# K and V loads whose 128 reads of 49152 B are each written as two pieces of 24576 B

## The chip, the core and the metric

The kernel runs on one core of a Trainium2 chip. The metric is the device time of one execution in microseconds (us); lower is better. The core has a matrix engine (PE, TensorE), VectorE (DVE), ScalarE (ACT), GpSimd (POOL) and SyncE (SP), each with an instruction stream of its own, and 16 DMA engines that move data between the chip's memory (HBM) and the on-chip memory of 128 partitions (SBUF). SP issues nearly all DMAs of this kernel.

## The reference

Two attention blocks, A and B, do the same thing on inputs of their own, and their outputs are joined along the last axis. Each takes one query token for each of 2 batch entries, and a cache of 8192 keys and values for each of 32 heads of width 192, in bf16.

```python
def _B_ref(x, k_cache, v_cache, wq, wo):
    B, Sq, D = x.shape                 # 2, 1, 640
    H, Dh = 32, 192                    # caches: 2 x 32 x 8192 x 192
    q = (x @ wq).reshape(B, Sq, H, Dh).transpose(0, 2, 1, 3)
    scores = jnp.einsum("bhqd,bhkd->bhqk", q, k_cache) * (Dh ** -0.5)
    p = _softmax(scores, axis=-1)
    o = jnp.einsum("bhqk,bhkd->bhqd", p, v_cache)
    return o.transpose(0, 2, 1, 3).reshape(B, Sq, H * Dh) @ wo
```

(Block A repeats its keys over head groups by a factor of one, so it is the same computation.) Nearly all of the data are the four caches: 4 x 2 x 32 x 8192 x 192 elements of 2 bytes, 805 MB, each read once.

## The kernel before

The work is cut into 64 steps, called pairs here after their two heads: a step takes two neighbouring heads of one batch entry of one block. The keys of two heads are one contiguous stretch of 6 MB (6,291,456 B) in HBM, and so are the values. `kv_src` (L189) views the stretch as 128 rows of 24576 elements (49152 B), one for each partition: partition 0 to 63 hold the first head, 64 to 127 the second, each partition with 128 tokens.

**Buffers.** There are three buffers `ring0` to `ring2` of 128 x 24576 bf16 (L138), 6 MB each. Loads take them in turn: `next_slot` (L196) counts 0, 1, 2, 0, ... The query weights `wq` of both blocks come first, then K and V of each pair in turn (the last two pairs have both K ahead of both V), then the output weights `wo` in pieces.

**Loads.** All these loads are issued by SP, in program order, through `load` and `load_on` (L181 to L187). A load waits until its buffer is free, and SP waits with it, so the loads behind it wait too. A K buffer is free once VectorE has made the fourth product from it (the mark `m, i, 3`), a V buffer once TensorE has run its 64 matmuls (the mark `pv, i`):

```python
            free[s] = [("m", i, 3)] if kind == "k" else [("pv", i)]
```

The consumers wait on the load's semaphore, of which each buffer has one (`rsem`), raised by 16 when a load has landed. The last V load is issued as two column halves of 128 x 12288 elements, so that TensorE can begin on the first half.

**A pair's computation.** The query of the two heads is copied to all partitions by a matmul with a selection matrix (L276) and rounded into `qt` (L282, L283). VectorE multiplies K by it in four quarters (`prod`, L291); TensorE sums 12 slices of each quarter into `scps` with an identity matrix (L296), and VectorE reduces the rest into the scores `sc` (L303). The maximum over the head goes through GpSimd (L312), ScalarE takes the exponentials into `pb` with their sums (L324), and TensorE multiplies them with V in 64 matmuls (L336). The division and the placing of the result (L359 to L379) follow in the next pair. Twelve matmuls on `filler` (L344) do no work that is used; they fill the time in which TensorE waits. The output projection (L394) comes after the last pair.

**Order.** Each engine has a list of operations (`_Stream`) with marks that others wait for, written out in the order of the program; 57 of the 64 pairs run in a loop of 19 turns of three pairs. SP's list is not in a loop.

Of the kernel before, what the change touches and what calls it, by code (L numbers as in the profile page):

```python
# [100 lines left out]
def build_kernel(nc, blocks, out):  # L101
# [15 lines left out]
    DC = D // 128  # L117
    N = Hn * Dh
    RW = T * Dh
    QC = 512  # L120
    NQC = N // QC
    NH2 = D // 2
# [5 lines left out]
    def pair(i):  # L128
        blk, r = divmod(i, B * PB)
        b, ii = divmod(r, PB)  # L130
        return blk, b, ii

    with ExitStack() as es:
# [3 lines left out]

        ring = [sb(f"ring{i}", [128, RW], BF16) for i in range(3)]  # L138
        prod = [sb(f"prod{i}", [128, TQ * Dh], BF16) for i in range(2)]
# [28 lines left out]
        reg = {}  # L168
        S_sp = _Stream("sp", sem("s_sp"), reg)
# [4 lines left out]
        rsem = [sem(f"rsem{i}") for i in range(3)]  # L174
# [4 lines left out]
        rcount = [0, 0, 0]  # L179

        def load(key, slot, out_ap, in_ap, waits):  # L181
            rcount[slot] += 16
            reg[key] = (rsem[slot], rcount[slot])
            load_on(out_ap, in_ap, rsem[slot], waits)

        def load_on(out_ap, in_ap, s, waits=()):
            S_sp.add(lambda eng, t: eng.dma_start(out_ap, in_ap).then_inc(s, 16), waits=waits)  # L187

        def kv_src(which, i):  # L189
            blk, b, ii = pair(i)  # L190
            return blocks[blk][which][b, 2 * ii:2 * ii + 2].rearrange("h s d -> (h s d)").rearrange("(p f) -> p f", p=128)

        slot_of = {}
        free = [[], [], []]

        def next_slot(n=[0]):  # L196
            n[0] += 1
            return (n[0] - 1) % 3

        for blk in range(NBLK):  # L200
            w = blocks[blk]["wq"].rearrange("(j c) n -> j (c n)", c=DC)
            s = next_slot()
            load(("wq", blk), s, ring[s][:], w[:, 0:RW], [])
            reg[("wq5", blk)] = (psem[blk], 16)
            load_on(prod[blk][:, 0:N], w[:, RW:RW + N], psem[blk])
            free[s] = [("pr", blk, NQC - 1)]
# [5 lines left out]
        for kind, i in order:  # L212
            s = next_slot()
            slot_of[kind, i] = s
            src = kv_src(kind, i)
            if (kind, i) == ("v", LAST):
                load((kind, i), s, ring[s][:, 0:RW // 2], src[:, 0:RW // 2], free[s])
                reg[("v2", i)] = (v2sem, 16)
                load_on(ring[s][:, RW // 2:RW], src[:, RW // 2:RW], v2sem)
            else:  # L220
                load((kind, i), s, ring[s][:], src, free[s])
            free[s] = [("m", i, 3)] if kind == "k" else [("pv", i)]

        wo_at = {}
# [28 lines left out]
        def add_proj(blk, n):  # L253
            def fn(eng, t):
                for c in range(DC):
                    src = ring[blk][:, c * N + n * QC:c * N + (n + 1) * QC] if c < DC - 1 else \
                        prod[blk][:, n * QC:(n + 1) * QC]
                    ins = eng.matmul(ops[n % 2][32 * blk:32 * blk + 2, 0:QC], xT[:, c, 2 * blk:2 * blk + 2], src,  # L258
                                     start=(c == 0), stop=(c == DC - 1))
# [3 lines left out]
                     sig=("pr", blk, n))  # L263
            S_act.add(lambda eng, t: eng.activation(qrow[32 * blk:32 * blk + 2, n * QC:(n + 1) * QC],
                                                 ops[n % 2][32 * blk:32 * blk + 2, 0:QC], ACTF.Identity),
                      waits=[("pr", blk, n), ("qz",)], sig=("qe", blk, n))
# [167 lines left out]
        def fn_x(eng, t):  # L434
            for c in range(DC):
# [4 lines left out]
                  waits=[("xp",)], sig=("xT",))  # L440
# [82 lines left out]
def bass_concat_heads__gqa_block_cached__mha_block_cached__decode_kernel(  # L523
    nc: bass.Bass,
    A_x: bass.AP,
    A_k_cache: bass.AP,
    A_v_cache: bass.AP,
    A_wq: bass.AP,
    A_wo: bass.AP,
    B_x: bass.AP,  # L530
    B_k_cache: bass.AP,
    B_v_cache: bass.AP,
    B_wq: bass.AP,
    B_wo: bass.AP,
    out: bass.AP,
):
    blocks = [
        dict(x=A_x, k=A_k_cache, v=A_v_cache, wq=A_wq, wo=A_wo),
        dict(x=B_x, k=B_k_cache, v=B_v_cache, wq=B_wq, wo=B_wo),
    ]  # L540
    build_kernel(nc, blocks, out)
# [28 lines left out]
```

## Time and profile before

| | |
|---|---|
| time, median of 3 runs | 1944.9 us (1944.57 to 1945.34) |
| time of the profiled execution | 1945.02 us |
| its span, first to last instruction | 1943.3 us |
| mean granted TensorE clock | 0.996 |
| TensorE matmul / VectorE / ScalarE / GpSimd busy | 84% / 56% / 10% / 2% |
| DMA, mean over the span | 431 GB/s, 837.03 MB |
| K or V load of 6 MB, issue to landing | 26.4 us / 29.2 us |

The profile is of one execution, which took 0.1 us more than the median of the runs without a profile. A busy share is an average over the span; what an engine waits for is in the waits, and how far the DMA engines are filled is in the DMA share by stretch. The time from issue to landing includes the time in which a load stands behind the load before it, so it is longer than the time in which its data move. The packet records of the trace give start, size and duration of every single transfer on a DMA engine: a row of 49152 B of a K or V load is one packet there.

### The profile page before, as it was taken

How to read it: one execution, taken by the hardware profiler on the slowest of the kernel's cores; microseconds unless marked ns; L12 is line 12 of the kernel's file. 1: busy time of each engine (PE TensorE's matmuls, PEld its weight loads, DVE VectorE, ACT ScalarE, POOL GpSimd, SP SyncE). 2: the span in 40 equal slices, each digit the busy share in tenths (PEclk: the TensorE clock that was granted, in tenths of full speed). 3: DMA queues.
4: the chain of work that ended last, by engine and by line, in shares of the span. 5: the costliest groups of instructions: out<-in, count | busy, mean ns of one | idle time of the engine just before them, and what ended most of it. 6: DMA issues, size and time to landing. Idle time of an engine off the chain costs nothing.

```text
span 1943.3 us, 21419 instructions
## 1 busy us (share of the span) xinstructions
PE 1630.2 (84%) x8639; PEld 786.8 (40%) x8703; DVE 1081.2 (56%) x834; ACT 187.1 (10%) x608; POOL 35.0 (2%) x88
## 2 busy tenths in 40 slices
PE   4888888888888888888888888888888888888888
PEld 1343443443443443443443443443443443443434
DVE  0556546546646646646656646645655645645660
ACT  2111011011011011011011011001001001001000
POOL 1000000000000000000000000000000000000000
PEclk9999999999999999999999999999999999999999
DMA  9999999999999999999999999999999999999998
GB/s 416 430 430 434 435 431 430 433 437 432 430 433 437 431 429 435 436 431 430 435 434 433 429 435 433 434 430 435 433 433 431 435 433 432 432 435 432 431 429 375
DMA packets 20777, 837.03 MB, mean 431 GB/s; under 512 B 2316, under 2 KB 2584, under 8 KB 2968
## 3 DMA queue, kind: packets, MB, share of 16 engines
q1 hardware_dynamic: 20744, 836.78, 99.8%
q8 instruction: 13, 0.21, 0.0%
q14 instruction: 4, 0.03, 0.0%
q10 hardware_dynamic: 16, 0.01, 0.0%
HBM read 836.77 MB, written 0.01 MB: 431 GB/s over the span
## 4 chain that ended last, share of the span: by engine, by line
issue 87%; PE 4%; DMA 4%; DVE 3%; POOL 1%; ACT 0%; SPq 0%; POOLq 0%; ACTq 0%; DVEq 0%
DVE prod L291 2%; PE ops L336 2%; DMA ring<-in_B_wq_dram 2%; DMA ring<-in_B_k_cache_dram 1%; POOL mg L312 1%; PE scps L296 1%; DMA ring<-in_B_wo_dram 1%; PE ops L258 1%; DVE sc L303 0%; PE outps L344 0%; ACT pb L324 0%; SPq L187 0%; PE outps L394 0%; POOLq L48 0%; DVE mp L309 0%
## 5 line engine op out<-in xcount | busy, mean ns | idle before, releaser
L291 DVE TENSOR_TENSOR prod<-ring,qt 128x6144 bf16<-128x6144 bf16 x256 | 852.6, 3351 | 696.3 <-DMA ring<-in_B_k_cache_dram 324.3
L296 PE MATMUL scps<-prod,ident 128*128 128x512 bf16 x3072 | 709.1, 381 | 210.0 <-DVE prod L291 210.0
L336 PE MATMUL ops<-ring,pb 128*34 128x384 bf16 x4096 | 676.8, 326 | 0.0
L296 PEld LDWEIGHTS scps<-prod,ident 128*128 128x128 bf16 x3072 | 280.3, 98 | 616.2 <-DVE prod L291 311.1
L336 PEld LDWEIGHTS ops<-ring,pb 128*34 128x34 bf16 x4096 | 395.5, 98 | 258.7
L303 DVE TENSOR_REDUCE sc<-scps 128x32 f32<-128x512 f32 x256 | 175.4, 685 | 108.8 <-PE scps L296 108.8
L344 PE MATMUL outps<-filler,ident 128*128 128x512 bf16 x704 | 162.4, 379 | 9.9 <-issue 9.8
L344 PEld LDWEIGHTS outps<-filler,ident 128*128 128x128 bf16 x768 | 70.1, 98 | 78.4
L359 ACT ACTIVATE oodd<-ops 2x192 f32<-2x192 f32 x64 | 20.6, 322 | 690.3 <-PE ops L336 690.3
L282 ACT ACTIVATE qt<-qps 64x192 bf16<-64x192 f32 x64 | 20.8, 324 | 663.9 <-PE qps L276 663.9
L324 ACT ACTIVATE pb<-sc,nb 64x128 bf16<-64x128 f32 x128 | 81.5, 637 | 7.6
L349 PE MATMUL ops<-ones,rs 128*2 128x1 f32 x128 | 12.2, 164 | 56.1 <-ACT pb L324 56.1
L312 POOL PARTITION_ALL_REDUCE mg<-mp x64 | 25.9, 404 | 1851.1 <-DVE mp L309 1851.1
L317 ACT ACTIVATE nb<-mg 64x1 f32<-64x1 f32 x64 | 13.0, 203 | 330.8 <-POOL mg L312 330.8
L349 PEld LDWEIGHTS ops<-ones,rs 128*2 128x2 f32 x128 | 5.5, 82 | 87.1 <-ACT pb L324 86.7
L324 ACT ACTIVATION_READ_ACCUMULATOR pb<-sc,nb 64x1 f32 x128 | 38.4, 300 | 0.0
L258 PE MATMUL ops<-ring,xT 128*2 128x512 bf16 x96 | 27.1, 409 | 6.6 <-issue 4.9
L276 PE MATMUL qps<-qrow,sel 34*128 (+1 forms) x64 | 21.3, 333 | 1.4 <-ACT qt L283 0.8
L379 PEld LDWEIGHTS oall<-on,place 2*128 (+1 forms) x256 | 10.3, 92 | 29.3 <-issue 26.3
L308 DVE TENSOR_REDUCE mp<-sc 64x1 f32<-64x128 f32 x64 | 17.8, 278 | 7.3
L363 DVE RECIPROCAL rc<-ops 2x1 f32<-2x1 f32 x64 | 9.4, 146 | 21.2 <-PE ops L336 21.2
L365 DVE TENSOR_TENSOR oodd<-ops,oodd 2x192 f32<-2x192 f32 x64 | 20.9, 326 | 0.4 <-ACT oodd L359 0.4
(41 smaller groups left out, 168.8 us busy)
## 6 DMA issues: line engine op xcount, KB each, us to landing
ring<-in_A_k_cache_dram SPq DMA_DIRECT2D x32, 6144.0 KB, 26.4
ring<-in_A_v_cache_dram SPq DMA_DIRECT2D x32, 6144.0 KB, 29.2
ring<-in_B_k_cache_dram SPq DMA_DIRECT2D x32, 6144.0 KB, 26.4
ring<-in_B_v_cache_dram SPq DMA_DIRECT2D x31, 6144.0 KB, 29.2
ring<-in_A_wq_dram SPq DMA_DIRECT2D x1, 6144.0 KB, 17.4
ring<-in_B_wq_dram SPq DMA_DIRECT2D x1, 6144.0 KB, 35.8
ring<-in_B_v_cache_dram SPq DMA_DIRECT2D x2, 3072.0 KB, 25.4
ring<-in_A_wo_dram SPq DMA_DIRECT2D x2, 3040.0 KB, 21.4
```

The costliest lines, as they stand in the source:

```text
L258: ins = eng.matmul(ops[n % 2][32 * blk:32 * blk + 2, 0:QC], xT[:, c, 2 * blk:2 * blk + 2], src, start=(c == 0), stop=(c == DC - 1))
L276: return eng.matmul(qps[:, 0:2 * Dh], sel[:].rearrange("p s m -> p (s m)")[:, bass.ds(k, 128)], qrow[:, bass.ds(c, 2 * Dh)], start=True, s ...
L282: eng.activation(qt[i % 3][0:64, :], qps[0:64, 0:Dh], ACTF.Identity)
L291: S_dve.add(lambda eng, t: eng.tensor_tensor(pr3(qd), quarter(i, qd), q, ALU.mult), waits=w, sig=("m", i, qd))
L296: ins = eng.matmul(scps[qd % 2][:], ident[:], pr3(qd)[:, :, j * DG:(j + 1) * DG], start=(j == 0), stop=(j == NJ - 1))
L303: S_dve.add(lambda eng, t: eng.tensor_reduce(sc[i % NB][:, qd * TQ:(qd + 1) * TQ], scps[qd % 2][:], AXL.X, ALU.add), waits=[("s", i, qd), ...
L312: S_pool.add(lambda eng, t: eng.partition_all_reduce(mg[i % NB][:], mp[i % NB][:], 128, bass.bass_isa.ReduceOp.max), waits=[("mx", i), key ...
L324: ins = eng.activation(pb[i % NB][p0:p0 + 64, :, h::32], sc[i % NB][p0:p0 + 64, :].rearrange("p (j a) -> p j a", a=2), ACTF.Exp, bias=nb[i ...
L336: ins = eng.matmul(ops[i % NB][0:34, 0:2 * Dh], pb[i % NB][:, j, :], vv[:, j, :], start=(j == 0), stop=(j == T // 2 - 1))
L344: ins = eng.matmul(outps[:], ident[:], filler[:], start=True, stop=True)
L359: S_act.add(lambda eng, t: eng.activation(oodd[i % NB][:], ops[i % NB][32:34, Dh:2 * Dh], ACTF.Identity), waits=[("pv", i), key("on", i - ...
L365: S_dve.add(lambda eng, t: eng.tensor_tensor(oodd[i % NB][:], ops[i % NB][0:2, 0:Dh], oodd[i % NB][:], ALU.add), waits=[("od", i)], sig=(" ...
```

## The change

K and V loads, apart from the last V load with its two halves, are issued by a new function `load_wide` in place of `load`. The source is described as 128 rows of 49152 B, as before. The destination is described as 128 partitions with two pieces of 24576 B each, one right behind the other, which are the same addresses as before. The DMA instruction is built directly, since the two descriptions have different piece sizes. The semaphore and its count, the wait for the free buffer, the order of loads and all other instructions stay.

```diff
+    RR = 128
+    WE = RW // 2
...
-        def kv_src(which, i):
+        def kv_flat(which, i):
             blk, b, ii = pair(i)
-            return blocks[blk][which][b, 2 * ii:2 * ii + 2].rearrange("h s d -> (h s d)").rearrange("(p f) -> p f", p=128)
+            return blocks[blk][which][b, 2 * ii:2 * ii + 2].rearrange("h s d -> (h s d)")
+
+        def load_wide(key, slot, i, waits):
+            rcount[slot] += 16
+            reg[key] = (rsem[slot], rcount[slot])
+            from_ap = kv_flat(key[0], i).rearrange("(p a f) -> p a f", p=RR, a=1)
+            to_ap = ring[slot][:].rearrange("p (a f) -> p a f", a=RW // WE)
+
+            def fn(eng, t):
+                ins = mybir.InstDMACopy(
+                    name=nc.get_next_instruction_name(), engine=mybir.EngineType.SP, queue="qSPDynamicHW",
+                    mode="Copy", ins=eng.lower_ap_dma(from_ap), outs=eng.lower_ap_dma(to_ap))
+                return eng.add_instruction(ins).then_inc(rsem[slot], 16)
+            S_sp.add(fn, waits=waits)
...
-            src = kv_src(kind, i)
+            src = kv_flat(kind, i).rearrange("(p f) -> p f", p=128)
             if (kind, i) == ("v", LAST):
...
             else:
-                load((kind, i), s, ring[s][:], src, free[s])
+                load_wide((kind, i), s, i, free[s])
```

## The prediction

> **What bounds the kernel now.** I read the page from the top, then the DMA share by stretch, the waits, the chain of one pair, the instructions on `ring`, and last the trace's records of single DMA packets (start, size, duration), which no line of the page prints. The page first:
>
> ```profile
> span 1943.3 us, 21419 instructions
> PE 1630.2 (84%) x8639; PEld 786.8 (40%) x8703; DVE 1081.2 (56%) x834; ACT 187.1 (10%) x608; POOL 35.0 (2%) x88
> ...
> DMA packets 20777, 837.03 MB, mean 431 GB/s; under 512 B 2316, under 2 KB 2584, under 8 KB 2968
> ...
> q1 hardware_dynamic: 20744, 836.78, 99.8%
> ...
> ring<-in_B_k_cache_dram SPq DMA_DIRECT2D x32, 6144.0 KB, 26.4
> ring<-in_B_v_cache_dram SPq DMA_DIRECT2D x31, 6144.0 KB, 29.2
> ```
>
> No engine is full, but SP's DMA queue (q1) holds all 16 DMA engines for 99.8% of the span. The stretches, with DMA share and GB/s in the last two columns, show where that isn't so:
>
> ```profile
> 0.00:100.00 100.00, 64.13 (x288) 26.87 (x290) 31.55 (x17) 19.93 (x41) 9.45 (x25) 0.95 0.99 423
> 100.00:1000.00 900.00, 767.45 (x4034) 371.65 (x4063) 522.49 (x404) 82.22 (x279) 10.99 (x31) 1.00 1.00 433
> 1000.00:1850.00 850.00, 723.80 (x3800) 349.88 (x3828) 492.20 (x385) 78.42 (x267) 10.64 (x30) 1.00 1.00 433
> ...
> 1900.00:1943.30 43.30, 34.08 (x318) 19.37 (x315) 1.61 (x6) 1.93 (x6) 0.00 (x0) 0.96 0.87 367
> ```
>
> From 100 to 1850 us the share is 1.00 at 433 GB/s; only the last 43 us fall short. The waits agree: VectorE idles 324.3 us for B's K loads, and a like time for A's:
>
> ```profile
> DVE prod L291 <- DMA ring<-in_B_k_cache_dram: 324.3, 31, 10.7
> DVE prod L291 <- DMA ring<-in_A_k_cache_dram: 318.2, 31, 11.1
> ```
>
> Two steps of the chain that ended last give the length of a pair:
>
> ```profile
> 1006.10 28.67 issue
> ...
> 1035.17 28.87 issue
> ```
>
> "Issue" is unexplained time here, so I take only the starts: 1035.17 - 1006.10 = 29.07 us for one K and one V load, 14.535 us a load. A load of 128 rows puts 8 rows on each of 16 engines, so a row takes 14.535 / 8 = 1817 ns. Every nanosecond added to a row reaches the end time.
>
> **The price of a row.** Among the packet records of the widest sizes, the shortest are 460 ns (12288 B), 912 ns (24576 B) and 1815 ns (49152 B). The differences are 452 ns for 12288 B and 903 ns for 24576 B, or 27.2 B per ns each time. What is left is 460 - 452 = 8 ns, 912 - 903.5 = 8.5 ns, 1815 - 1807 = 8 ns: a packet costs its bytes at 27.2 B/ns and a fixed 8 ns, whatever its length. The means are 915.7 ns (256 packets of 24576 B) and 1820.6 ns (16512 of 49152 B). A semaphore packet of 4 B is recorded as 9 ns, and in the steady stretch the next row on the engine starts 6 ns after it: 6 ns is what the smallest piece holds its engine.
>
> **What the change does, part by part.** Bytes, places, semaphores, slot order and waits stay. Removed: 127 `dma_start` loads (128 K and V loads, less the last V, which stays in two column halves). Added: 127 loads whose source is still 128 rows of 49152 B and whose destination is 128 x 2 pieces of 24576 B. Per engine 127 x 8 = 1016 rows get one more write piece each. The compiled program of the changed kernel carries 128x2x12288 elements as the destination on SP and holds the same instructions in the same order on the other engines.
>
> SP's issue. Here are the issues of B's loads in the instructions on `ring` (shortest/median/longest ns):
>
> ```profile
> L187 SPq DMA_DIRECT2D ring<-in_B_v_cache_dram x33: 327/328/740, 972.6 to 1874.0; - x33
> L187 SPq DMA_DIRECT2D ring<-in_B_k_cache_dram x32: 327/328/328, 960.6 to 1844.5; - x32
> ```
>
> An issue takes 0.33 us. A K load lands 26.4 us after issue and moves for 14.5, so it is issued 11.9 us before the engines come to it. Were the issue twice as long for twice the pieces, 0.33 us would lie inside 11.9 us: zero. Without that cover it would be 127 x 0.33 = 42 us. Only the wait for a slot stands behind it on SP, and the following load has the same lead. Nothing else is queued past it.
>
> The write piece. No row shows one read feeding two writes, so I bound it. Upper end: the row behaves as two packets of 24576 B; by means 2 x 915.7 - 1820.6 = 10.8 ns, times 1016 = 11.0 us, by the fixed part 8 ns x 1016 = 8.1 us. Lower end: the fixed 8 ns belongs to something that the split takes away, and all of it goes: -8.1 us. Between them, if the 8 ns belong to the read alone and a second write opens while data flow: 0. I take the nearest thing to a bare extra piece, the semaphore packet: 6 ns x 1016 = 6.1 us. I choose it over 8 because the read of the row isn't opened a second time, and over 0 because reads and writes run at the same 27.2 B/ns, so there is no spare rate on the writing side to make up a lost 6 ns.
>
> **The sum.** The profiled execution took 1945.02 us, its span 1943.3 and 1.7 around it; the median of three runs is 1944.9, so one base serves: 1945.0 + 6.1 = 1951.1 us, 0.31% slower. Between 8.1 and 11.0 of the upper end it would be 1953.1 to 1956.0. Compute can't become the bound in this: VectorE has 324.3 / 31 = 10.5 us of idle time in a pair.
>
> [...]
>
> **The rivals.**
>
> *The read sets the row's price, the write is free.* Then the added pieces cost between 0 and, with a little of the 6 ns showing, 3.9 us: 1945.0. For it: the fixed 8 ns are seen only where a new read starts too, so the trace can't give it to the write. Against: the equal rates above. Here belongs also that the change doesn't do what it says: the two pieces adjoin in the partition, and if whatever makes the pieces on the chip joined them again, the time is 1945.0 as well. [...]
>
> *The row becomes two packets.* If the hardware cuts reads to the size of the writes, the price is 8.1 us by the fixed part: 1953.1. For it: by the access patterns every data packet in the trace has one read and one write of equal size. Against: nothing that asks for the cut; the access pattern keeps 128 reads.
>
> *A load runs as one stream* (the faster side). Once reads and writes no longer come in equal pairs, the engine may not close each row by itself, but take the 8 reads and 16 writes of its share as one packet. Seven of eight fixed parts go: 7 x 8 = 56 ns a load, times 127 = 7.1 us, 1937.9. It decides as soon as rows follow each other with less than 8 ns between, and then beats the 6 ns per piece wherever the pieces open while data flow. For it: with 1817 ns a row against 1807 for its bytes there are 10 ns to win. Against: rows are the packets of the trace now, and nothing here shows a packet of several. [...]
>
> *The engine stalls between the pieces.* The first rows of the program, with no data under way, took 2.4 to 3.2 us in place of 1.8; if each second piece waited like that for some 0.6 us, 1016 x 0.6 = 610 us come on top, 2555 us. Against: semaphore packets, also tiny writes between rows, hold their engine for 6 ns only.
>
> **How the numbers follow.** The measurement can tell about 0.2% (3.9 us) from no change. The write piece at some 6 ns: 0.42. Two packets: 0.18. Stall: 0.03. These are slower, 0.63. Free write or joined pieces: 0.20, the same. One stream: 0.17, faster. The forecast is the likeliest, 1951.1. The range must leave out no more than 2 in 10: the top takes in both upper bounds, 1956.0; the bottom takes in the free write at 1945.0 and half of the largest gain (8.1 / 2), 1940.9. The stall and the rest of the one-stream case stay outside.
>
> **What would show it.** In the changed profile: a pair of 29.07 + 16 x 0.006 = 29.17 us in the chain, 431.5 GB/s where it says 433 now, the K loads landing as before plus a tenth, the DMA share still 1.00. If q1 counts 20744 packets, a row is still one packet, and its mean length against 1820.6 ns gives the price of a piece directly; 16256 more packets (127 x 128) of 24576 B say two packets. Wrong it would be with an unchanged 29.07 us (the read sets the price), with a pair under 29.0 us (one stream), or with a DMA share under 1.00 in the middle stretches (stalls, or SP's issue no longer covered).

## The result and the profile after

The changed kernel takes 1954.0 us (median of 6 runs, 1953.48 to 1954.29) against 1944.7 (6 runs, 1944.57 to 1945.34). The ratio is 1.0048, with a 95% interval of 1.0037 to 1.0058: it is slower by 9.3 us. The profiled execution took 1953.98 us.

The page of the changed kernel, in the lines that answer to those of before:

```profile
span 1952.2 us, 21483 instructions
PE 1641.5 (84%) x8703; PEld 786.9 (40%) x8703; DVE 1081.2 (55%) x834; ACT 187.0 (10%) x608; POOL 35.1 (2%) x88
...
DMA packets 20777, 837.03 MB, mean 429 GB/s; under 512 B 2316, under 2 KB 2584, under 8 KB 2968
...
q1 hardware_dynamic: 20744, 836.78, 99.8%
...
ring<-in_B_k_cache_dram SPq DMA_DIRECT2D x32, 6144.0 KB, 26.7
ring<-in_B_v_cache_dram SPq DMA_DIRECT2D x31, 6144.0 KB, 29.4
```

VectorE and ScalarE have the busy time that they had; PE's 64 further matmuls (x8703 for x8639) are records that the profile of before lacks, since the program has the same ones. q1 has 20744 packets, not one more: a row of 49152 B is still one packet record. The queue is as full as before and moves less in a microsecond. The same in the stretches (DMA share and GB/s in the last two columns):

```profile
0.00:100.00 100.00, 65.50 (x292) 27.12 (x292) 32.46 (x17) 19.93 (x41) 9.47 (x25) 0.97 0.99 422
100.00:1000.00 900.00, 768.44 (x4046) 370.04 (x4046) 517.15 (x402) 82.22 (x279) 11.05 (x31) 1.00 1.00 431
1000.00:1850.00 850.00, 724.11 (x3808) 348.02 (x3806) 491.12 (x380) 76.91 (x261) 10.33 (x29) 1.00 1.00 431
...
1909.00:1952.20 43.20, 35.00 (x319) 19.67 (x317) 1.62 (x6) 1.93 (x6) 0.00 (x0) 0.96 0.89 373
```

The loss is spread over the loads, 431 GB/s in place of 433. Behind the loads nothing is lost: from the issue of the last V load's second half to the end pass 1952.2 - 1883.2 = 69.0 us, where it was 1943.3 - 1874.0 = 69.3. Two steps of the chain that ended last, one pair apart:

```profile
1010.48 28.81 issue
...
1039.69 29.01 issue
```

A pair takes 1039.69 - 1010.48 = 29.21 us where it took 29.07. That is 0.14 us for 16 rows of an engine, 8.8 ns a row. The packet records say nearly the same: a row of 49152 B took 1820 ns in the median and takes 1829 now (1820.6 and 1829.4 in the mean). 1016 rows x 9 ns are 9.1 us; the measured 9.3 us are 9.1 ns a row. VectorE waits longer for K, by 4.9 us in block B and 7.2 in block A, and a little less elsewhere:

```profile
DVE prod L306 <- DMA ring<-in_B_k_cache_dram: 329.2, 31, 11.2
DVE prod L306 <- DMA ring<-in_A_k_cache_dram: 325.4, 31, 11.0
```

And SP's issues, among the instructions on `ring` (shortest/median/longest ns):

```profile
L205 SPq DMA_DIRECT2D ring<-in_B_k_cache_dram x32: 539/540/540, 964.7 to 1853.0; - x32
L205 SPq DMA_DIRECT2D ring<-in_B_v_cache_dram x31: 539/540/541, 976.8 to 1870.2; - x31
...
L189 SPq DMA_DIRECT2D ring<-in_B_v_cache_dram x2: 336/710/1085, 1882.8 to 1883.2; - x2
```

An issue grew from 328 to 540 ns. It stays inside the lead that a load has over its transfer, 26.7 us from issue to landing less 14.6 of moving; the share of 1.00 agrees with this: in these stretches the DMA engines were never short of work.

### The profile page after: what moved, and what is told of

Read it like the earlier page. It is cut to its first block, busy times and chain, and to the rows that moved or that the text cites. A ratio compares the mean times of both kernels' runs of the same rounds, so it can differ in the third digit from the quotient of the medians.

```text
span 1952.2 us, 21483 instructions
## 1 busy us (share of the span) xinstructions
PE 1641.5 (84%) x8703; PEld 786.9 (40%) x8703; DVE 1081.2 (55%) x834; ACT 187.0 (10%) x608; POOL 35.1 (2%) x88
## 3 DMA queue, kind: packets, MB, share of 16 engines
q1 hardware_dynamic: 20744, 836.78, 99.8%
## 4 chain that ended last, share of the span: by engine, by line
issue 87%; PE 5%; DMA 3%; DVE 3%; POOL 1%; ACT 0%; SPq 0%; POOLq 0%; ACTq 0%; DVEq 0%
DVE prod L306 2%; PE ops L351 2%; PE ops L273 2%; DMA ring<-in_B_k_cache_dram 1%; POOL mg L327 1%; DMA prod<-in_A_wq_dram 1%; PE scps L311 1%; DMA ring<-in_B_wo_dram 1%; DVE sc L318 0%; PE outps L359 0%; ACT pb L339 0%; SPq L189 0%; POOLq L48 0%; PE outps L409 0%; DVE mp L324 0%
## 5 line engine op out<-in xcount | busy, mean ns | idle before, releaser
L359 PE MATMUL outps<-filler,ident 128*128 128x512 bf16 x768 | 176.9, 380 | 0.0
## 6 DMA issues: line engine op xcount, KB each, us to landing
ring<-in_A_k_cache_dram SPq DMA_DIRECT2D x32, 6144.0 KB, 26.7
ring<-in_B_k_cache_dram SPq DMA_DIRECT2D x32, 6144.0 KB, 26.7
```

The lines of the kernel that those rows point to most:

```text
L359: ins = eng.matmul(outps[:], ident[:], filler[:], start=True, stop=True)
```

## The experiments

The diffs are against the changed kernel. The question is what the 9.1 ns belong to: the further write piece, a row whose reads and writes don't pair off, the read, or the way the DMA is issued.

### How the price grows with the pieces: 4, 16 and 64 of them

```diff
-    WE = RW // 2
+    WE = RW // 4      # RW // 16 and RW // 64 in the others
```

Expected with four pieces:

> 128 reads of 49152 B, four write pieces of 12288 B for each (127 loads, 8 rows per engine). The changed kernel costs 9.3 us for one more piece on 1016 rows of an engine, 9.1 ns a piece. Theory A, every further write piece costs its engine its own 9.1 ns: three further pieces, 1944.7 + 3 x 9.3 = 1972.6 us, a row packet of about 1820 + 27 = 1847 ns. Theory B, a row pays once for reads and writes that do not pair off: 1954.0 us, 1829 ns. Theory C, the writes of a row have to exceed the read's own fixed 8 ns first (17 ns for two pieces, 8.5 each): 4 x 8.5 - 8 = 26 ns, 1971 us. SP's issue grows from 540 to about 960 ns and stays hidden, the DMA share 1.00.

Expected with sixteen:

> 128 reads of 49152 B, sixteen write pieces of 3072 B for each. Theory A: 15 x 9.3 = 139.5, 2084 us, a row of 1820 + 15 x 9.1 = 1957 ns. Theory B: 1954.0 us. Theory C: 16 x 8.5 - 8 = 128 ns a row, 1016 x 128 = 130 us, 2075 us. Rival D, the price hangs on the size of a piece (a part of it is a share of the bytes): anything well off these lines. Issue by 212 ns per piece of a row: 0.33 + 15 x 0.21 = 3.5 us, under the load's lead of 12 us, so still hidden; were it not hidden, the DMA share in the middle would fall under 1.00.

Expected with 64:

> 128 reads of 49152 B, 64 write pieces of 768 B each. Theory A: 63 x 9.53 = 600 us, 2545 us, a row of 1820 + 63 x 9.4 = 2412 ns, 19.3 us a load, DMA share 1.00. Rival H: with this many pieces SP's issue, which in the run with 16 pieces took up to 3.5 us, becomes longer than a load moves, the engines run dry: over 2545 us, with a DMA share under 1.00 in the middle. Rival D: small pieces cost more each than 9.4 ns, with the share still 1.00.

| pieces of a row | bytes of one | median us | more than before | for each further piece | row packet, median ns |
|---|---|---|---|---|---|
| 1 (before) | 49152 | 1944.7 | | | 1820 |
| 2 (the change) | 24576 | 1954.0 | 9.3 | 9.3 | 1829 |
| 4 | 12288 | 1973.2 | 28.5 | 9.5 | 1848 |
| 16 | 3072 | 2087.7 | 143.0 | 9.5 | 1961 |
| 64 | 768 | 2546.5 | 601.7 | 9.55 | 2415 |

The line is straight from 1 to 63 further pieces. In the last row 601.7 / 63 = 9.55 us a piece, over 1016 rows 9.4 ns. A price paid once for a row (B) would have stayed at 1954.0, so it falls. Theory C gave 2075 us for sixteen pieces and A 2084; 2087.7 is nearer to A, and above it by 0.2 us a piece, because A's 9.3 came from a single piece. With 64 pieces C would be at 64 x 8.5 - 8 = 536 ns a row, 2489 us, and the run took 2546.5. At these sizes the price doesn't hang on the size of a piece (D): those of 768 B cost 9.55 us each in the time, those of 12288 B 9.5.

The runs with 16 and 64 pieces were also to show whether SP's issue can become the bound (H). With 16, the stretches and the longest issues:

```profile
100.00:1000.00 900.00, 725.98 (x3742) 349.62 (x3768) 480.59 (x373) 76.92 (x261) 10.34 (x29) 0.98 1.00 402
1000.00:1850.00 850.00, 693.79 (x3521) 332.13 (x3549) 459.42 (x353) 71.61 (x243) 9.62 (x27) 0.97 1.00 402
```

```profile
L205 SPq DMA_DIRECT2D ring<-in_A_v_cache_dram x32: 539/1589/3526, 37.8 to 1012.5; - x32
```

With 64:

```profile
100.00:1000.00 900.00, 622.22 (x3018) 292.86 (x3042) 399.97 (x305) 60.96 (x207) 8.15 (x23) 0.88 1.00 326
1000.00:1850.00 850.00, 591.52 (x2871) 278.09 (x2890) 374.86 (x287) 58.33 (x199) 7.79 (x22) 0.89 1.00 326
```

```profile
L205 SPq DMA_DIRECT2D ring<-in_A_k_cache_dram x32: 643/19120/19721, 2.9 to 1212.9; - x32
...
L205 SPq DMA_DIRECT2D ring<-in_B_v_cache_dram x31: 16745/17299/19195, 1273.1 to 2446.7; - x31
```

SP now stands 17 to 19 us in an issue, about as long as a load moves (8 rows of 2415 ns, 19.3 us), and yet the DMA share is 1.00 and the time lies on the line. So the time shows no price of the issue, up to 19.7 us of it. Could a row be longer because its engine waits for SP between the pieces? With two and four pieces SP is done with an issue after 0.54 us, some 12 us before the engines come to its load, and a piece costs the same there as with 64. So it isn't SP that holds the rows up; what takes the 9.4 ns is not in the traces. With four pieces an issue still took 540 ns; the growth "by 212 ns per piece" in the expectation was wrong.

### Reads cut as well

```diff
-            from_ap = ....rearrange("(p a f) -> p a f", p=RR, a=1)
+            from_ap = ....rearrange("(p a f) -> p a f", p=RR, a=2)   # a=4 in the third
```

Two reads and two pieces for a row:

> 256 reads of 24576 B and 256 write pieces of 24576 B: the row is cut on both sides. Theory A, only the write pieces cost, a second read nothing: the same as the changed kernel, 1954.0 us. Rival E, reads and writes pay each for itself: 9.3 + 8.1 (the fixed part of a packet of the kernel before), 1962 us. Rival F, only the read sets the price and the changed kernel's hardware had cut its reads too: also 1954.0, but then the changed kernel would show 24576 B packets, which it does not. Theory B, unequal pairing costs: only the fixed part of a further packet, 1952.8 us. Packets of 24576 B, 912 to 916 ns each.

Two reads and four pieces (with `WE = RW // 4` as well):

> 256 reads of 24576 B, four write pieces of 12288 B for each 49152 B: twice the reads of the kernel with 128 reads and four pieces, the same writes. Theory A: equal to that kernel, 1972.6 us. Rival E (a read pays too): 8.1 us more, 1980.7. Theory B: 256 unequal rows pay 9.3 each over the kernel with 256 equal ones, about 1953 + 18.6 = 1971 us, and then the kernel with 128 reads and four pieces stands at 1954.

Four reads and four pieces (`a=4` and `WE = RW // 4`):

> 512 reads of 12288 B and 512 write pieces of 12288 B in one DMA: the third step of the row of runs with four write pieces (one, two and now four reads for each 49152 B). Theory A: reads beside as many writes cost nothing, 1973.2 as with one and two reads. Rival E, a read costs as soon as there are as many reads as writes: 1973.2 + 2 x 8.1 = 1989 us.

| reads of a row | pieces | median us | q1 packets |
|---|---|---|---|
| 1 | 2 (the change) | 1954.0 | 20744 |
| 2 | 2 | 1954.2 | 37000 |
| 1 | 4 | 1973.2 | 20744 |
| 2 | 4 | 1973.2 | 37000 |
| 4 | 4 | 1973.3 | 69512 |

From the pages of the runs with two reads and two pieces, and four and four, the line of q1 (packets, MB, share):

```profile
q1 hardware_dynamic: 37000, 836.78, 100.0%
```

```profile
q1 hardware_dynamic: 69512, 836.78, 100.4%
```

The number of packet records follows the reads: 16256 more for one more read of each row (127 x 128), and none for two or four pieces at one read. The time doesn't follow them. It follows the pieces written, within 0.2 us. Rival E, a price for reads beside that for writes, is refuted up to as many reads as writes. No run has more reads than writes, so two things stay open: what a read costs that no write covers, and whether the price belongs to the write as such or to whichever of the two sides has more pieces.

### Only the K loads

```diff
-                load_wide((kind, i), s, i, free[s])
+                (load_wide((kind, i), s, i, free[s]) if kind == "k" else
+                 load((kind, i), s, ring[s][:], src, free[s]))
```

> The two write pieces on the 64 K loads only, the V loads as before the change: 64 x 8 = 512 further pieces for each engine in place of 1016. Theory A (every write piece costs 9.4 ns by the runs with 4 and 16 pieces): 512 x 9.4 = 4.8 us, 1949.5. Rival G, the price comes from the instruction built by hand or its longer issue (540 ns in place of 328), one of them in each pair being enough to show it or to hide it: 1944.7 or 1954.0.

1949.4 us (10 runs), a ratio of 1.0024 (1.0014 to 1.0034): 4.7 us for 512 further pieces, 9.1 ns each. Half the dose is half the effect, and no load shows or hides another's. This alone doesn't clear the instruction built by hand or its longer issue, since a price for each such load would be halved too. The runs around it do: the line through 2, 4, 16 and 64 pieces, all built by hand, comes back at one piece to 1954.0 - 9.55 = 1944.5 us, the time of the plain loads (1944.7); and the next run has four plain DMAs in place of one built by hand, at the same time.

### What a semaphore packet costs

The prediction had taken a semaphore packet for a bare write. This run adds 381 of them to each engine at the same reads and pieces as the kernel with four of each:

```diff
-    WE = RW // 2
+    WE = RW // 4
...
-            rcount[slot] += 16
+            rcount[slot] += 64
...
+            from_ap = kv_flat(key[0], i).rearrange("(p f) -> p f", p=RR)
+            for c in range(4):
+                load_on(ring[slot][:, c * WE:(c + 1) * WE], from_ap[:, c * WE:(c + 1) * WE], rsem[slot], waits)
```

> Each K and V load as four plain DMAs of 128 x 12288 B (column quarters), on the same semaphore, which is raised four times: the same 512 reads and 512 write pieces as the kernel with four of each, and three more semaphore packets on each engine for a load, 381 in all. By the 6 ns that the prediction read for a semaphore packet: 2.3 us more than that kernel, 1975.5 if it stands at 1973.2. If a semaphore packet costs its engine about 1 ns net, because the row after it is recorded 5 ns shorter: 1973.6. SP issues four times 0.33 us for a load, inside the load's lead of 12 us.

1973.6 us (1973.25 to 1973.72) beside 1973.3 (1973.16 to 1973.49) of that kernel: 0.3 us for 381 packets, 0.7 ns each, and hardly to be told from none. At 6 ns it would have been 2.3 us. So the 6 ns weren't a price. In the records of the changed kernel the row behind a semaphore is 1824 ns long in place of 1829: five of the six come back at once. And four plain issues a load (432 ns in the median) take the time of one built by hand (602 ns).

## Why the prediction was right, and where its size was off

**The bound** held: the share of 1.00 and the wait for K were right, and a cost on the DMA engines' rows came out at the end nearly one to one, up to 64 pieces: 595 ns more a row are 604.5 us in 1016 rows, and the time grew by 601.7.

**SP's issue at nothing** held, by a lead of some 12 us as worked out. Its length was guessed as doubling with the pieces; it is 540 ns for two and for four pieces, 212 ns more than before.

**The write piece** is the mis-sized term: forecast 6 ns, 6.1 us; measured 9.1 ns, 9.3 us. The step that failed is the choice of the row. The semaphore packet seemed the barest piece, but the start of the next packet is no measure of what a packet costs when the next one is shorter for it (1824 ns in place of 1829): a semaphore packet's cost in the time is about 0.7 ns, so the nearness of its 6 ns to the write piece's 9.1 is chance. Other rows at hand were nearer. The fixed part of 8 ns from three sizes gave 8.1 us. The step from row to row, 1817 ns against 1807 for the bytes, was named under the one-stream rival as "10 ns to win"; it gives 10.2 us, and it is free of the 3 ns by which records overlap (below). The means gave 11.0. The result lies among these, and the stated range held because its top took in the two upper bounds, not through the 6 ns. The reason for taking the piece at more than nothing, no spare rate on the writing side, was argued and not read from a row: a packet record gives one rate, 27.2 B/ns, for both sides. The runs agree with it, as each piece adds its whole price, but they don't show why.

**The packet count** doesn't set the price: it stayed at 20744 while the time grew by 9.3 us, and the kernel with 69512 packets runs as the one with 20744 at equal pieces (1973.3 and 1973.2 us). The trace records one packet for each read, so it can't show whether the engine counts in another way. What the runs show is some 9.4 ns for each further write.

**The rivals.** The free write (1945.0) is refuted, and with it the doubt whether the chip joins the pieces. Two packets (1953.1) had nearly the right time for a wrong reason: q1 kept its count, and a row its one record of 1829 ns. Two true packets take the same time (1954.2) with the same two writes. One stream (1937.9) would have had a pair under 29.07 us; it is 29.21. A stall of 0.6 us a piece isn't there, even with 64 pieces (9.4 ns each). (The first row of each engine, from which it was read, took 2.0 to 3.2 us, not 2.4 to 3.2.)

**What would show it:** a pair of 29.17 us was forecast, 29.21 came; 431.5 GB/s, 431 came; the mean row of 1829.4 ns against 1820.6 gave 8.8 ns, near the 9.1 that the time gives. From issue to landing K takes 0.3 us more, not 0.1. That fits the ring, though no run tests it: a buffer gets its next load three loads later, and three loads, each 0.07 us longer, make 0.2 us.

## What to carry to other kernels

Where the DMA engines are the bound, as here, count the pieces that are written, for one engine: in these runs each further one cost 9.1 to 9.4 ns beside its bytes, at sizes from 24576 down to 768 B, with as many reads or fewer. So a load should write the longest piece that its destination allows (here a partition's whole row, as in the kernel before); halving its pieces of 49152 B cost this kernel 0.5%, cutting them to 768 B cost it 31%. The number of packets on the page followed the reads (20744 with one read of a row, 37000 with two, at two pieces as at four) and tells nothing about this price; the length of a row's packet (1829 ns for 1820) and the GB/s of a full stretch (431 for 433) do. And to price a small thing from packet records, take the step between starts over many rows, or a run with more of that thing, rather than the gap beside a single packet.

## What the runs showed of the hardware that was not expected

- Reads cost nothing that shows beside as many writes: four times the reads of a row change the time by 0.1 us in 1973.
- With 9.4 ns for its one piece, a load of before comes to 8 x (1807 + 9.4) ns = 14.53 us, which is what its chain shows (14.535). That the first piece costs what further ones do fits, but isn't shown by itself, for no row can be without a piece.
- A semaphore packet, recorded at 9 ns, costs its engine about 0.7 ns (0.3 us for 381).
- An issue on SP took 328 ns for a plain load of one read and one piece a row (432 in the run with four plain DMAs a load), 540 for one read with two or four pieces, 602 where both are cut (as in the run with two reads and two pieces), 540 to 3526 with 16 pieces and up to 19.7 us with 64, with no loss of time in any. What SP waits for in the last two is not in the traces.
- Shares over 100% (100.4% with 69512 packets) fit records that overlap: in the steady stretch of the kernel before and of the changed one a packet starts some 3 ns ahead of the end of the one before it on its engine, and 48768 further packets on 16 engines, 3 ns each, are 9.1 us, 0.5% of the span.
